# Local attention and two feed-forward networks in one kernel: the low parts of the second network made by VectorE in a written order, and the sigmoid's table loaded at another place

## The chip, the cores and the metric

The kernel runs on one core of a Trainium2 chip. The metric is the device time of one launch in microseconds, as the median of several runs. One execution was also recorded by the hardware profiler; its times are counted from the start of its span.

## The reference, cut to what matters

Attention over 512 local and 32 global positions of 4 batches and 8 heads is followed by two feed-forward networks. The first has a layer norm, a hidden layer of 2048 with ReLU and a residual. The second is this:

```python
def _moe2_ref(x, w_in, conv_w, w_out):          # x (4, 544, 512)
    h = np.maximum(x @ w_in, 0.0)               # (4, 544, 1024)
    hp = pad(h, 1 position at each end)
    conv_out = sum(conv_w[k] * hp[:, k:k + S, :] for k in range(3))
    gate = 1.0 / (1.0 + np.exp(-conv_out))
    return h * gate @ w_out                     # (4, 544, 512)
```

All is in 32-bit floats. The kernel's attention yields 544 positions a batch (`S`), the global ones first.

## The kernel before, in words

Products on TensorE use operands that are split in two: a high part, which is a rounded copy, and a low part, the remainder. Three products (high by high, high by low, low by high) replace one. The helper `split(hi, lo, src, e_hi, e_lo)` (L112) makes both: a copy on engine `e_hi` (ScalarE throughout the second network, L108) and a subtraction on engine `e_lo` (L115). The low parts are the subject here.

The work runs in three stages that overlap: attention, the first network (over chunks of positions, `first_network`, L694) and, from about 540 us, the second network. The first network's hidden products are L711, their ReLU copies `hh` L720 (ScalarE) and `hl` L721 (VectorE), and its output products L735 to L740. While its last chunk runs, the second network's weights are prepared: `narrow` (L124) turns 64-bit words into floats with one Prelu on ScalarE (L131) and two operations on VectorE, and `w1_pair` (L795) forms sums and high and low parts of them.

The second network takes each batch's input `y` (512 features by 544 positions) from memory (`y_load`, into tile `yT`). The first product, `x @ w_in`, is done by a scheme with seven products for eight: features and positions are cut in halves, `y_sums` (L903) makes four sums on VectorE, and `y_split` (L915) splits seven operands, named B11, T2, T3, T1, T4, B21 and B22, into tiles `yc`. The operands T3, T4 and B22 get their low parts from GpSimd, the others from VectorE.

The 1024 hidden features are 8 blocks `f` of 128; two blocks, an even (E) and an odd one (O), are a pair `p`, four pairs a batch (`NPR`). `hidden(b, p, at)` (L1022) works on one pair, n = 4b + p. TensorE makes seven products of six matmuls each (L1005) into the PSUM banks `px`, `py`, `pv` and `pz`, each bank twice or so in a pair. ScalarE copies the first (`p1s`, L1037), VectorE adds the others up (L1032: `u2`, `u3`, and `e1`, `e0`, `o1`, which are the halves of the hidden tiles `he` and `ho`). An addition must have read a bank before TensorE's next product may write there. ScalarE does ReLUs (`relu0`, `relu`, `relu1`).

`gate(b, f, h, e)` (L1007) then does for each block: tap 0 on ScalarE (L1009, named `tap`), taps 1 and 2 on VectorE (L1011, named `(1, b, f)` and `(2, b, f)`), the sigmoid on ScalarE (L1013, `sig`), the product with h on VectorE (L1014, `mul`), and the split into `gh` (ScalarE) and `gl` (engine `e`: GpSimd, and VectorE in the very last pair). GpSimd copies the first 32 columns of both aside (L1018, L1019). There are two buffers `c`, four `gh` and four `gl`. `output` (L1089) multiplies gh and gl by `w_out` (L1077 to L1079), four tiles of twelve matmuls in all for each block; the blocks of pair n are multiplied while pair n + 2 is worked on, after its fourth product and after its seventh. The first two pairs have no such products beside them. At the end of a batch TensorE's results go through ScalarE to memory (L1098).

What sets the order: TensorE executes in the order in which the code is written (`keep_order`). On the other engines a scheduler picks, by priorities that follow the order of the code and by its own estimates of times; `ahead(n)` raises a priority, and `HEAD` (L779) is a list of names whose instructions must follow each other in that order, one list for VectorE and one for ScalarE. Instructions that the list does not name may come between. The four sums of the next batch are named `("sum", b, k)`, and the transposes of the first network's last two result tiles (VectorE, L688) `("turn", (3, 2))` and `("turn", (3, 3))`; each transpose is followed by four stores on SP's queue (L692) to the scratch memory from which batch 3's `y` is read.

The sigmoid needs another table on ScalarE than the functions before it. A sigmoid of one element, `sgd` (L1103), brings the load of that table to a chosen place: behind the last Prelu (`mark["prelu"]`).

Of the kernel before, what the change touches and what calls it, by code (L numbers as in the profile page):

```python
# [12 lines left out]
AF = mybir.ActivationFunctionType  # L13
ALU = mybir.AluOpType
# [4 lines left out]
B, H, SL, SG, D = 4, 8, 512, 32, 64  # L19
# [3 lines left out]
NF, NF2, NDC = FF // P, F2 // P, DM // P  # L23
# [40 lines left out]
def f32(ap):  # L64
    return ap.bitcast(F32)
# [3 lines left out]
def tile_kernel(ctx: ExitStack, tc: tile.TileContext, a_w, a_x, a_e, a_m, g_qk, g_v, w12, g_ln, w_in, w_out, conv_w, out):  # L69
# [42 lines left out]
    def split(hi, lo, src, e_hi, e_lo):  # L112

        copy(e_hi, hi, src)
        e_lo.tensor_tensor(lo, src, f32(hi), op=ALU.subtract)  # L115


    wt, wraw = {}, {}
    mark = {}

    def behind(e):

        return tc.issue_after(mark[e]) if e in mark else nullcontext()
# [319 lines left out]
    order, tiles = [], []  # L443
# [318 lines left out]
    def tick(k):  # L762
# [7 lines left out]
        if ci == 0:  # L770
# [5 lines left out]

    B_ADD = 300
    E0, O0, E1, O1, E2 = ((0, f) for f in range(5))
    HEAD = [  # L779
        [("u3", 0), ("e1", 0), ("e0", 0), ("o1", 0), (1, *E0), ("u2", 1), (2, *E0), ("u3", 1), ("e1", 1), (1, *O0),  # L780
         ("mul", *E0), ("e0", 1), ("turn", (3, 2)), (2, *O0), ("o1", 1), ("mul", *O0), ("turn", (3, 3)), ("u2", 2), (1, *E1), ("u3", 2), ("e1", 2), (2, *E1),
         (1, *O1), ("mul", *E1), ("e0", 2), ("sum", 0, 3), (2, *O1), ("sum", 0, 2), ("o1", 2), ("sum", 0, 1), ("mul", *O1),
         ("sum", 0, 0), (1, *E2), ("u2", 3), (2, *E2), ("u3", 3), ("e1", 3), ("mul", *E2)],
        [("p1s", 0), ("relu0", 0), ("relu", 0), ("tap", *E0), ("p1s", 1), ("relu1", 0), ("tap", *O0), ("sig", *E0),
         ("relu0", 1), ("relu", 1)],
    ]
    NPR = NF2 // 2
    EIGHTH = NDC * P // 2
    HB = S // 2
    zpools = []  # L790
# [4 lines left out]
    def w1_pair(p, home, raw, ab, sums, e):  # L795

        odd, even = 2 * p + 1, 2 * p
        st = {}
        cols = {odd: slice(0, DM), even: slice(DM, 2 * DM)}

        def load(f):
            st[f] = raw(f)
            SP.dma_start(st[f], w_in[f].bitcast(I32))

        def start(f):
            if f == odd:
                st["ab"] = ab()
            fp = st["ab"][:, cols[f]]
            st["o", f] = narrow(fp, st.pop(f), fp)
            mark["prelu"] = st["o", f][0]().ins  # L810

        def homes():
            st["s"] = sums()
            a, x = home()
            wae.append(a)
            wx.append(x)

        def sum_(k):
            a11, a12, a21, a22 = (st["ab"][:, i * EIGHTH:(i + 1) * EIGHTH] for i in range(4))
            s3, s2, s4 = (st["s"][:, i * EIGHTH:(i + 1) * EIGHTH] for i in range(3))  # L820
            o, i0, i1, op = [(s3, a11, a21, ALU.subtract), (a21, a21, a22, ALU.add), (s2, a22, s3, ALU.subtract),
                             (s4, a12, s2, ALU.subtract)][k]
            e.tensor_tensor(o, i0, i1, op=op)

        def hi(w, src, c):
            return lambda: ACT.activation(w[p][:, 0, c], st[src][:, c], AF.Copy)

        def lo(w, src, c, e):
            return lambda: e.tensor_tensor(w[p][:, 1, c], st[src][:, c], f32(w[p][:, 0, c]), op=ALU.subtract)

        a, b, x = cols[odd], cols[even], slice(0, 3 * EIGHTH)
        convs = [[lambda f=f: start(f)] + [lambda f=f, k=k: st["o", f][k]() for k in (1, 2)] for f in (odd, even)]
        rest = [homes, lambda: sum_(0), hi(wae, "ab", a), lambda: sum_(1), lambda: sum_(2), lo(wae, "ab", a, DVE),
                lambda: sum_(3), hi(wae, "ab", b), hi(wx, "s", x), lo(wae, "ab", b, DVE), lo(wx, "s", x, e)]
        return lambda f: lambda: load(f), convs, rest
# [76 lines left out]
                lambda: DVE.tensor_tensor(b12, b12, b11, op=ALU.subtract),  # L912
                lambda: DVE.tensor_tensor(t4, b21, t2, op=ALU.subtract)]

    def y_split(n):  # L915
        split(*yc[n], ysrc[n], ACT, POOL if Y_NAMES.index(n) in (2, 4, 6) else DVE)


    free = "xe" if last % 2 else "xo"
# [12 lines left out]

    def y0_split(n):
        y_home(n)
        y_split(n)

    raws = []

# [65 lines left out]
                with behind(key):  # L1004
                    PE.matmul(ps, wx_, y[:, d], start=start and d + m == 0, stop=d + m == 3, skip_group_check=True)  # L1005

    def gate(b, f, h, e):  # L1007
        c = gpool.tile([P, S], F32, tag="c", name="c")
        named["tap", b, f] = ACT.activation(c, h[:, 0:S], AF.Copy, scale=cw[:, 3 * f:3 * f + 1])  # L1009
        for k in (1, 2):  # L1010
            named[k, b, f] = DVE.scalar_tensor_tensor(c, h[:, k:S + k], cw[:, 3 * f + k:3 * f + k + 1], c, op0=ALU.mult,  # L1011
                                                      op1=ALU.add)
        named["sig", b, f] = ACT.activation(c, c, AF.Sigmoid)  # L1013
        named["mul", b, f] = DVE.tensor_tensor(c, h[:, 1:S + 1], c, op=ALU.mult)  # L1014
        gh = gpool.tile([P, S], F32R, tag="gh", name="gh", bufs=4)
        gl = gpool.tile([P, S], F32R, tag="gl", name="gl", bufs=4)
        split(gh, gl, c, ACT, e)
        POOL.tensor_copy(grem_h[:, f, b * SG:(b + 1) * SG], f32(gh[:, :SG]))  # L1018
        POOL.tensor_copy(grem_l[:, f, b * SG:(b + 1) * SG], f32(gl[:, :SG]))  # L1019
        gts[b, f] = gh, gl  # L1020

    def hidden(b, p, at):  # L1022

        a, x = wae[p], wx[p]
        n = b * NPR + p
        he, ho = hs[2 * n % 4], hs[(2 * n + 1) % 4]
        p1s, u2, u3 = (us[:, n % 2 * 3 + i] for i in range(3))
        e = DVE if n == B * NPR - 1 else POOL

        def add(name, o, i0, i1):  # L1030
            with ahead(B_ADD):
                named[name, n] = DVE.tensor_tensor(o, i0, i1, op=ALU.add)  # L1032

        px = ps_x.tile([P, HB], F32, tag="px", name="px")
        product(px, a, 0, "B11", True, "first")
        with ahead(B_ADD):
            named["p1s", n] = ACT.activation(p1s, px, AF.Copy)  # L1037
        at("B11")
        py = ps_x.tile([P, HB], F32, tag="py", name="py")
        product(py, x, 1, "T2", True, "first")  # L1040
        add("u2", u2, py, p1s)
        at("T2")
        pv = ps_v.tile([P, HB], F32, tag="pv", name="pv")
        product(pv, x, 0, "T3", True)
        add("u3", u3, pv, u2)
        at("T3")
        pz = ps_v.tile([P, HB], F32, tag="pz", name="pz")
        product(pz, a, 2, "T1", True)
        add("e1", he[:, U1], pz, u3)
        at("T1")  # L1050
        at(0)

        def t4():
            product(pv, a, 3, "T4", False)
            add("e0", he[:, U0], pv, u2)
            named["relu", n] = ACT.activation(he[:, 1:1 + S], he[:, 1:1 + S], AF.Relu)
            at("T4")

        def b21():
            product(px, a, 1, "B21", False)  # L1060
            with ahead(B_ADD):
                named["relu0", n] = ACT.activation(ho[:, U0], px, AF.Relu)
            at("B21")

        for part in (b21, t4) if n < 2 else (t4, b21):
            part()
        gate(b, 2 * p, he, e)
        product(pz, x, 2, "B22", False)
        add("o1", ho[:, U1], pz, u2)
        named["relu1", n] = ACT.activation(ho[:, U1], ho[:, U1], AF.Relu)  # L1070
        at("B22")
        gate(b, 2 * p + 1, ho, e)
        at(1)

    def mm_o(o, gh, gl, f, first, last):
# [23 lines left out]

    steps = [(b, f) for b in range(B) for f in range(NF2)]  # L1100
    second = len(traced())
    with behind("prelu"):
        ACT.activation(sgd, mhalf, AF.Sigmoid)  # L1103
    gpool.tile([P, S], F32R, tag="gl", name="gl", bufs=4)
    yT, sums = None, []
    for i in range(B * NPR):
        b, p = divmod(i, NPR)
        if p == 0 and b + 1 < B:
            yT = [(gpool.tile([P, NDC, S], F32, tag="yT", name="yT", bufs=1), slice(0, NDC))]
            y_load(b + 1, yT)  # L1110
        if p == 2 and b + 1 < B:
            sums = y_sums(yT, yt)

        def at(n):
            if n in (0, 1):
                if 2 * i >= 4:
                    output(*steps[2 * i - 4 + n])
            else:
                for _ in range(len(sums) if p == NPR - 1 else min(len(sums), 1)):
                    named["sum", b, len(sums)] = sums.pop(0)()  # L1120
                if b + 1 < B and p == NPR - 1:
                    y_split(n)

        hidden(b, p, at)
    for st in steps[-4:-1]:
# [6 lines left out]
        (ACT if b % 2 else SP).dma_start(out[b, :SG, :], orem[b * SG:(b + 1) * SG])  # L1132
    output(*steps[-1])
    keep_order(second, [mybir.EngineType.PE])
    for order in HEAD + [[("e0", NPR * b + 2), ("sum", b, 3)] for b in range(1, B - 1)]:
        order = [named[k].ins for k in order]
        for one, two in zip(order, order[1:]):
            tc.add_manual_dep(two, one.name, mybir.DependencyInfo(
                mybir.DependencyClass.NoSync, mybir.DependencyReason.DATA), reason="order")
# [103 lines left out]
```

## Time and profile before

| what | value |
|---|---|
| time, median of 3 runs | 736.89 us (736.3 to 737.52) |
| profiled execution, its own time | 736.67 us |
| its span, first to last instruction | 734.9 us |
| TensorE busy | 717.2 us (98% of the span) |
| VectorE busy | 497.0 us (68%) |
| ScalarE busy | 399.4 us (54%) |
| GpSimd busy | 241.3 us (33%) |

In the rows of the profile PE is TensorE's matmuls, PEld its weight loads, DVE VectorE, ACT ScalarE, POOL GpSimd, and SPq the queue of SyncE, which only issues transfers. In rows of busy time by stretch the engines stand in the order PE, PEld, DVE, ACT, POOL. An arrow reads "written from". A bracket at a row's end is the idle time of the engine ahead of it and what ended that.

### The profile page before, as it was taken

Reading aid. Unit: us, or ns where it says so; the run is one execution under the profiler, and the core shown is the slowest. Engines: PE = TensorE matmul, PEld = TensorE weight load, DVE = VectorE, ACT = ScalarE, POOL = GpSimd, SP = SyncE. Lnnn points to the kernel's source line nnn. Section 1 sums busy time; section 2 is a strip of 40 time slices with the busy share of each in tenths; the row PEclk is TensorE's granted clock in tenths of the full one; section 3 lists DMA queues with packets and bytes.
Section 4 is the critical chain, followed back from the end, with each engine's and each line's share of the span. In section 5 each row is a group of like instructions: output and inputs, shape, how many; then the busy total and the mean of one; then the engine's idle time right before and its main releaser. Section 6 shows DMA issues by size and latency. Waiting matters only on the chain.

```text
span 734.9 us, 12936 instructions
## 1 busy us (share of the span) xinstructions
PE 717.2 (98%) x4665; PEld 642.9 (87%) x4665; DVE 497.0 (68%) x1108; ACT 399.4 (54%) x927; POOL 241.3 (33%) x287
## 2 busy tenths in 40 slices
PE   9989999999999999999999999999999899999997
PEld 5878799999999999999999999989988788998886
DVE  3889982857677676756557534744859978778661
ACT  5858653455565656545445531523655576466551
POOL 1012031334354543434324410001343745417320
PEclk9999999999999999999999999999999999999999
DMA  9992231532443353243224102307311110110102
GB/s 370 425 415 85 71 136 52 110 98 84 117 106 97 98 126 104 87 124 93 83 74 108 44 23 32 112 30 235 141 62 30 62 57 1 62 58 1 59 0 72
DMA packets 64160, 76.19 MB, mean 104 GB/s; under 512 B 39120, under 2 KB 46048, under 8 KB 61536
## 3 DMA queue, kind: packets, MB, share of 16 engines
q1 hardware_dynamic: 31888, 70.59, 28.8%
q10 hardware_dynamic: 32208, 4.77, 3.9%
q8 instruction: 37, 0.61, 0.3%
q14 instruction: 27, 0.22, 0.1%
HBM read 66.43 MB, written 8.91 MB: 103 GB/s over the span
## 4 chain that ended last, share of the span: by engine, by line
PE 75%; DVE 15%; issue 4%; ACT 3%; DMA 3%; ACTq 0%; SPq 0%; DVEq 0%
PE ph L711 21%; PE yps L735 7%; PE yps L736 7%; PE yps L740 7%; PE po L337 3%; PE pt L316 3%; DVE c L1011 3%; PE po L1078 3%; PE po L1077 3%; PE po L1079 3%; PE pz L1005 2%; PE pv L1005 2%; DMA wraw<-w_in 2%; PE px L1005 2%; PE pog L422 1%
## 5 line engine op out<-in xcount | busy, mean ns | idle before, releaser
L711 PE MATMUL ph<-xe,w 128*128 128x256 f32 (+1 forms) x768 | 119.4, 298 | 0.9 <-ACT w L159 0.9
L711 PEld LDWEIGHTS ph<-xe,w 128*128 128x128 f32 x768 | 108.9, 188 | 6.7 <-ACT w L159 1.2
L115 POOL TENSOR_TENSOR kl<-raw,kh 128x448 fp32r<-128x448 f32 (+2 forms) x59 | 70.0, 1186 | 131.0 <-ACT kh L108 124.3
L735 PE MATMUL yps<-w,hh 128*128 128x512 f32 x272 | 110.2, 405 | 2.4 <-ACT hh L720 1.8
L711 PE MATMUL ph<-xo,w 128*128 128x256 f32 x768 | 108.6, 285 | 0.0
L736 PE MATMUL yps<-w,hh 128*128 128x512 f32 x272 | 107.8, 396 | 0.0
L711 PEld LDWEIGHTS ph<-xo,w 128*128 128x128 f32 x768 | 101.7, 190 | 4.4
L720 ACT ACTIVATE hh<-ph 128x256 fp32r<-128x256 f32 (+1 forms) x128 | 50.3, 394 | 70.6 <-PE ph L711 54.4
L721 DVE SCALAR_TENSOR_TENSOR hl<-ph,hh 128x256 fp32r<-128x256 f32 x112 | 46.4, 416 | 49.5 <-ACT hh L720 49.0
L740 PE MATMUL yps<-w,hl 128*128 128x512 f32 x224 | 73.0, 400 | 0.0
L294 DVE CUSTOM_DVE_ANT_0 sm<-ps,mask 128x192 f32<-128x192 f32 (+1 forms) x128 | 42.5, 368 | 36.4 <-PE ps L291 24.8
L115 POOL TENSOR_TENSOR gl<-c,gh 128x544 fp32r<-128x544 f32 x30 | 43.2, 1439 | 70.8 <-ACT gh L108 61.0
L303 ACT ACTIVATE sm<-sm,nm 128x192 f32<-128x192 f32 (+1 forms) x128 | 58.7, 460 | 12.4 <-DVE nm L294 12.1
L1011 DVE SCALAR_TENSOR_TENSOR c<-hs,cw,c 128x544 f32<-128x544 f32 x64 | 58.3, 935 | 3.3 <-ACT c L1009 2.0
L735 PEld LDWEIGHTS yps<-w,hh 128*128 128x128 f32 x272 | 51.2, 188 | 9.5 <-ACT hh L720 2.8
L736 PEld LDWEIGHTS yps<-w,hh 128*128 128x128 f32 x272 | 51.4, 189 | 5.5
L108 ACT ACTIVATE kh<-raw 128x448 fp32r<-128x448 f32 (+2 forms) x59 | 34.3, 582 | 39.6 <-issue 17.1
L1078 PE MATMUL po<-w,gh 128*128 128x512 f32 x128 | 50.7, 396 | 0.0
L1077 PE MATMUL po<-w,gh 128*128 128x512 f32 x128 | 50.6, 395 | 0.0
L1079 PE MATMUL po<-w,gl 128*128 128x512 f32 x128 | 50.5, 395 | 0.0
L261 POOL TENSOR_TENSOR qs<-raw,qs 64x256 fp32r<-64x256 f32 x43 | 33.6, 783 | 46.3 <-DVE qs L260 21.2
L740 PEld LDWEIGHTS yps<-w,hl 128*128 128x128 f32 x224 | 41.0, 189 | 8.6 <-DVE hl L721 0.3
(187 smaller groups left out, 1503.8 us busy)
## 6 DMA issues: line engine op xcount, KB each, us to landing
wraw<-w SPq DMA_DIRECT2D x16, 1024.0 KB, 16.9
raw<-a_m SPq DMA_DIRECT2D x23, 352.0 KB, 3.0
raw<-a_e SPq DMA_DIRECT2D x20, 320.0 KB, 2.9
raw<-g_qk SPq DMA_DIRECT2D x16, 304.0 KB, 2.8
rawg<-g_v SPq DMA_DIRECT2D x16, 280.0 KB, 2.9
wraw<-w_in SPq DMA_DIRECT2D x8, 512.0 KB, 6.2
wraw<-w_out SPq DMA_DIRECT2D x4, 1024.0 KB, 7.6
raw<-a_w SPq DMA_DIRECT2D x4, 912.0 KB, 9.7
```

Of the source, the lines that this page charges most:

```text
L115: e_lo.tensor_tensor(lo, src, f32(hi), op=ALU.subtract)
L303: ACT.activation(s, s, AF.Exp, bias=self.nm[:, j:j + 1], scale=-1.0, accum_out=xt.sums[:, h:h + 1])
L711: e = PE.matmul(ph[:, :n], w[:, d * P:(d + 1) * P], x[:, d], start=m == 0, stop=m == 3 * NDC - 1)
L720: ACT.activation(hh, ph[:, :n], AF.Relu)
L721: DVE.scalar_tensor_tensor(hl, ph[:, :n], 0.0, f32(hh), op0=ALU.max, op1=ALU.subtract)
L735: PE.matmul(yps[i], hh[:, tk], wh[:, DM:], start=edge(k, -1), stop=False)
L736: PE.matmul(yps[i], hh[:, tk], wl[:, DM:], start=False, stop=False)
L740: mark["last"] = PE.matmul(yps[i], hl[:, tk], wh[:, DM:], start=False, stop=edge(k, 1)).ins
L1011: named[k, b, f] = DVE.scalar_tensor_tensor(c, h[:, k:S + k], cw[:, 3 * f + k:3 * f + k + 1], c, op0=ALU.mult, op1=ALU.add)
L1077: PE.matmul(o, gh, wh, start=first, stop=False)
L1078: PE.matmul(o, gh, wl, start=False, stop=False)
L1079: PE.matmul(o, gl, wh, start=False, stop=last)
```

## The change

The low parts of the second network's gates and of its `yc` operands for batches 1 to 3 all go to VectorE; batch 0's `yc`, made during the first network, stay as they were. `HEAD` is written anew: VectorE's list names the low parts (`lo`) of the first four blocks, puts `u3` right behind `u2` and `o1` right behind `e0`, and the two transposes move to a list of their own, behind `e0` of pairs 5 and 6. For batches 1 and 2 two short lists put `yc` T3 and the product of block 4 behind `u3` and `e1` of the batch's last pair. The one-element sigmoid is no longer tied to the last Prelu; ScalarE's list puts it between `p1s` and `relu0` of pair 0.

```diff
@@ split
-        e_lo.tensor_tensor(lo, src, f32(hi), op=ALU.subtract)
+        return e_lo.tensor_tensor(lo, src, f32(hi), op=ALU.subtract)
@@ HEAD
+    NPR = NF2 // 2
     HEAD = [
-        [("u3", 0), ("e1", 0), ("e0", 0), ("o1", 0), (1, *E0), ("u2", 1), (2, *E0), ("u3", 1), ("e1", 1), (1, *O0),
-         ("mul", *E0), ("e0", 1), ("turn", (3, 2)), (2, *O0), ("o1", 1), ("mul", *O0), ("turn", (3, 3)), ("u2", 2), (1, *E1), ("u3", 2), ("e1", 2), (2, *E1),
-         (1, *O1), ("mul", *E1), ("e0", 2), ("sum", 0, 3), (2, *O1), ("sum", 0, 2), ("o1", 2), ("sum", 0, 1), ("mul", *O1),
-         ("sum", 0, 0), (1, *E2), ("u2", 3), (2, *E2), ("u3", 3), ("e1", 3), ("mul", *E2)],
-        [("p1s", 0), ("relu0", 0), ("relu", 0), ("tap", *E0), ("p1s", 1), ("relu1", 0), ("tap", *O0), ("sig", *E0),
+        [("u3", 0), ("e1", 0), ("e0", 0), ("o1", 0), (1, *E0), ("u2", 1), ("u3", 1), (2, *E0), ("e1", 1), (1, *O0),
+         ("mul", *E0), ("e0", 1), ("o1", 1), (2, *O0), ("lo", *E0), ("u2", 2), ("u3", 2), ("mul", *O0), ("e1", 2),
+         (1, *E1), (2, *E1), ("lo", *O0), (1, *O1), ("mul", *E1), ("e0", 2), (2, *O1), ("sum", 0, 3), ("o1", 2),
+         ("lo", *E1), ("sum", 0, 2), ("mul", *O1), ("sum", 0, 1), ("sum", 0, 0), ("u2", 3), ("u3", 3), (1, *E2), ("e1", 3),
+         (2, *E2), ("lo", *O1)],
+        [("p1s", 0), ("sgd",), ("relu0", 0), ("relu", 0), ("tap", *E0), ("p1s", 1), ("relu1", 0), ("tap", *O0), ("sig", *E0),
          ("relu0", 1), ("relu", 1)],
+        [("e0", NPR + 1), ("turn", (3, 2)), ("e0", NPR + 2), ("turn", (3, 3))],
     ]
@@ w1_pair
-            mark["prelu"] = st["o", f][0]().ins
+            st["o", f][0]()
@@ y_split, y0_split
-    def y_split(n):
-        split(*yc[n], ysrc[n], ACT, POOL if Y_NAMES.index(n) in (2, 4, 6) else DVE)
+    def y_split(n, e=DVE):
+        return split(*yc[n], ysrc[n], ACT, e)
...
-        y_split(n)
+        y_split(n, POOL if Y_NAMES.index(n) in (2, 4, 6) else DVE)
@@ gate, hidden
-    def gate(b, f, h, e):
+    def gate(b, f, h):
...
-        split(gh, gl, c, ACT, e)
+        named["lo", b, f] = split(gh, gl, c, ACT, DVE)
...
-        e = DVE if n == B * NPR - 1 else POOL
...
-        gate(b, 2 * p, he, e)
+        gate(b, 2 * p, he)
...
-        gate(b, 2 * p + 1, ho, e)
+        gate(b, 2 * p + 1, ho)
@@ the loop over pairs
-    with behind("prelu"):
-        ACT.activation(sgd, mhalf, AF.Sigmoid)
+    named["sgd",] = ACT.activation(sgd, mhalf, AF.Sigmoid)
...
-                    y_split(n)
+                    named["yc", b, n] = y_split(n)
...
-    for order in HEAD + [[("e0", NPR * b + 2), ("sum", b, 3)] for b in range(1, B - 1)]:
+    for order in HEAD + [[("e0", NPR * b + 2), ("sum", b, 3)] for b in range(1, B - 1)] + [
+            [("u3", NPR * b + 3), ("e1", NPR * b + 3), e] for b in range(1, B - 1) for e in (("yc", b, "T3"), ("mul", b, 4))]:
```

## Rows read from the trace of the kernel before

**Rows 1.** Busy time by stretch: start:end, length, engines (instructions), granted clock, DMA share, GB/s.

```profile
549.50:580.00 30.50, 26.50 (x164) 23.30 (x163) 29.87 (x42) 19.06 (x36) 14.92 (x15) 1.00 0.12 18
```

**Rows 2.** TensorE's waits from 515 to 735: us in total, times, longest.

```profile
PE pv L1005 <- DVE us L1032: 3.1, 2, 2.7
PE pz L1005 <- DVE hs L1032: 2.9, 3, 1.0
```

**Rows 3.** Timeline around the table load: start, duration, engine, line, operation.

```profile
533.74 1.28 ACT L1103 ACT_TABLE_LOAD   x1
...
535.14 0.36 ACT L720 ACTIVATE hh<-ph 128x256 fp32r<-128x256 f32 x1
...
535.56 0.50 PE L735 MATMUL yps<-w,hh 128*128 128x512 f32 x1 [1.79 <-ACT hh L720]
```

**Rows 4.** Timeline of TensorE: the first product of pairs 2, 4, 8, 11 and 12.

```profile
553.36 0.92 PE L1005 MATMUL px<-yc,wae 128*128 128x272 f32 x6
...
580.09 0.92 PE L1005 MATMUL px<-yc,wae 128*128 128x272 f32 x6
...
625.34 0.91 PE L1005 MATMUL px<-yc,wae 128*128 128x272 f32 x6
...
658.09 0.91 PE L1005 MATMUL px<-yc,wae 128*128 128x272 f32 x6
...
670.24 0.91 PE L1005 MATMUL px<-yc,wae 128*128 128x272 f32 x6
```

**Rows 5.** Busy time by stretch, behind the idle time of rows 3.

```profile
536.00:540.00 4.00, 4.00 (x18) 3.58 (x17) 2.61 (x3) 1.07 (x4) 3.87 (x8) 0.57 0.01 2
```

**Rows 6.** Timeline of GpSimd, VectorE and TensorE around 554 to 557.

```profile
554.34 1.36 POOL L115 TENSOR_TENSOR gl<-c,gh 128x544 fp32r<-128x544 f32 x1 [9.79 <-PE px L1005]
...
554.46 1.82 DVE L1011 SCALAR_TENSOR_TENSOR c<-hs,cw,c 128x544 f32<-128x544 f32 x1
...
556.20 0.43 DVE L1032 TENSOR_TENSOR hs<-pz,us 128x272 f32<-128x272 f32 x1
...
556.68 1.01 PE L1005 MATMUL pz<-yc,wae 128*128 128x272 f32 x6 [0.90 <-DVE hs L1032]
```

**Rows 7.** Timeline of VectorE and TensorE around 572 to 575.

```profile
572.50 1.85 DVE L1011 SCALAR_TENSOR_TENSOR c<-hs,cw,c 128x544 f32<-128x544 f32 x1
...
574.75 1.03 PE L1005 MATMUL pv<-yc,wae 128*128 128x272 f32 x6 [2.70 <-DVE us L1032]
```

**Rows 8.** Timeline of ScalarE in pair 0: `p1s` and `relu0`.

```profile
542.52 0.38 ACT L1037 ACTIVATE us<-px 128x272 f32<-128x272 f32 x1
546.75 0.40 ACT L1062 ACTIVATE hs<-px 128x272 f32<-128x272 f32 x1 [3.85 <-PE px L1005]
```

**Rows 9.** Instructions on tile `c`: count, ns min/median/max, first and last start, form.

```profile
L1011 DVE SCALAR_TENSOR_TENSOR c<-hs,cw,c x64: 772/784/1900, 549.5 to 714.2; 128x544 f32<-128x544 f32 x64
...
L108 ACT ACTIVATE gh<-c x32: 642/659/685, 553.6 to 716.5; 128x544 fp32r<-128x544 f32 x32
L115 POOL TENSOR_TENSOR gl<-c,gh x30: 1352/1367/1862, 554.3 to 707.2; 128x544 fp32r<-128x544 f32 x30
L115 DVE TENSOR_TENSOR gl<-c,gh x2: 719/722/726, 716.3 to 717.2; 128x544 fp32r<-128x544 f32 x2
```

**Rows 10.** Groups of VectorE in 549.5 to 580: count, busy us, mean ns, idle before.

```profile
L1011 DVE SCALAR_TENSOR_TENSOR c<-hs,cw,c 128x544 f32<-128x544 f32 x12 | 14.4, 1203 | 0.8 <-ACT c L1009 0.8
```

**Rows 11.** Timeline of VectorE at the end of batch 1.

```profile
619.40 1.88 DVE L115 TENSOR_TENSOR yc<-yT,yc 128x544 fp32r<-128x544 f32 x1
621.21 0.43 DVE L1032 TENSOR_TENSOR hs<-pz,us 128x272 f32<-128x272 f32 x1
```

**Rows 12.** Timeline of SP's queue: stores of y, stores of the output, load of batch 3.

```profile
554.57 5.74 SPq L692 DMA_DIRECT2D yscr<-x  x8
...
601.11 2.98 SPq L1098 DMA_DIRECT2D out<-osb  x4
626.82 0.38 SPq L888 DMA_DIRECT2D yT<-yscr  x1
```

More of the change, by code (lines that the diff above doesn't have):

```diff
@@ L778, in tile_kernel @@
     E0, O0, E1, O1, E2 = ((0, f) for f in range(5))
+    NPR = NF2 // 2
     HEAD = [
-        [("u3", 0), ("e1", 0), ("e0", 0), ("o1", 0), (1, *E0), ("u2", 1), (2, *E0), ("u3", 1), ("e1", 1), (1, *O0),
-         ("mul", *E0), ("e0", 1), ("turn", (3, 2)), (2, *O0), ("o1", 1), ("mul", *O0), ("turn", (3, 3)), ("u2", 2), (1, *E1), ("u3", 2), ("e1", 2), (2, *E1),
-         (1, *O1), ("mul", *E1), ("e0", 2), ("sum", 0, 3), (2, *O1), ("sum", 0, 2), ("o1", 2), ("sum", 0, 1), ("mul", *O1),
-         ("sum", 0, 0), (1, *E2), ("u2", 3), (2, *E2), ("u3", 3), ("e1", 3), ("mul", *E2)],
-        [("p1s", 0), ("relu0", 0), ("relu", 0), ("tap", *E0), ("p1s", 1), ("relu1", 0), ("tap", *O0), ("sig", *E0),
+        [("u3", 0), ("e1", 0), ("e0", 0), ("o1", 0), (1, *E0), ("u2", 1), ("u3", 1), (2, *E0), ("e1", 1), (1, *O0),
[4 more added lines that the diff above has]
+        [("p1s", 0), ("sgd",), ("relu0", 0), ("relu", 0), ("tap", *E0), ("p1s", 1), ("relu1", 0), ("tap", *O0), ("sig", *E0),
          ("relu0", 1), ("relu", 1)],
+        [("e0", NPR + 1), ("turn", (3, 2)), ("e0", NPR + 2), ("turn", (3, 3))],
     ]
-    NPR = NF2 // 2
     EIGHTH = NDC * P // 2
```

## The prediction

> **What bounds the kernel now.** I read the busy shares in stretches first. TensorE is the engine that counts: it has no free stretch except around the start of the second network. In 549.5 to 580 it is busy 26.50 of 30.50 us, while VectorE is busy 29.87 of them [rows 1]: there VectorE sets the pace. Then TensorE's waits from 515 on: five for VectorE, 6.0 us together, two before `pv` and three before `pz` [rows 2]. Those are PSUM banks that an addition of `hidden` has not yet read. A sixth, for ScalarE, stands ahead of the second network [rows 3]. The timeline then says what each addition stood behind.
>
> TensorE's own steady pace is the yardstick. From 625.34 to 658.09 three pairs pass with no wait: 10.92 us a pair [rows 4]. Against it, pairs 2 and 3 (553.36 to 580.09) take 26.73 instead of 21.83, 4.9 too many; pairs 4 to 7 (580.09 to 625.34) 45.25 instead of 43.67, 1.6 too many; pair 11 (658.09 to 670.24) 12.15, 1.2 too many [rows 4]. These 7.7 us contain the five waits and the restart of the pipeline behind each. With what the sixth wait costs, this is all that a better order on the other engines could win.
>
> **The table load.** ScalarE loads the sigmoid's table from 533.74; the ReLU copy `hh` that TensorE needs next starts at 535.14 and TensorE goes on at 535.56, after 1.79 us idle [rows 3]. Without the load `hh` can start at 533.74: **1.40 us** less, and 0.39 us of idle time stays, since a Prelu ahead of it is late anyway. [...]
>
> The load goes behind `p1s` of pair 0. There ScalarE has nothing from 542.90 to 546.75, when `relu0` gets its operand: 3.85 us of cover [rows 8] for 1.40. [...] Without cover it would cost its 1.40 before `relu0`.
>
> [...]
>
> [...]
>
> **Low parts from GpSimd to VectorE.** 30 `gl` at 1.37 us on GpSimd become 30 at 0.72 on VectorE [rows 9]; nine `yc` low parts have the same shape, so the same price. That adds 39 x 0.72 = 28 us to VectorE. What comes back: taps (`scalar_tensor_tensor`) take 0.78 undisturbed and up to 1.90 [rows 9]. The row to look at is the tap at 554.46: 1.82 us, behind a GpSimd subtraction that began at 554.34 and ran 1.36 [rows 6]. [...] In 549.5 to 580 twelve taps take 1.20 on the mean [rows 10], 12 x 0.42 = 5.0 us too many. Added in the same stretch are five `gl` (E0 to E2) and about two `yc`: 7 x 0.72 = 5.0 us. So even in the worst stretch the balance is nil before the two transposes that leave it, and GpSimd keeps only its short copies of 32 columns. VectorE's load over a batch: a pair has 5 additions of 0.43 [rows 6], 4 taps of 0.78, two low parts of 0.72 and two products of the same shape [rows 9], 8.15 us; a batch adds four sums and seven `yc`, 7.9: 4 x 8.15 + 7.9 = 40.5 against TensorE's 43.7. It fits. What the move costs on the path is nothing by this; it is covered by TensorE's own products.
>
> A low part now stands in VectorE's queue behind a copy `gh` of 0.66 us [rows 9], and behind it wait the additions that free TensorE's banks. The written order puts other work between product and low part; only in `lo O0`, then tap 1 of O1, a hand-over to ScalarE and back is open (the tap needs the buffer that `lo` frees): about 0.75 us, at a point where the next addition is due some 2 us later. I charge nothing, at most 0.9.
>
> **The written order.** Each wait of rows 2 has its cause in what stands before an addition, and the new list takes it away.
> - `o1` of pair 1 ends at 556.63, TensorE waits 0.90 [rows 6]. In front of it stood a transpose and the slow tap; now it follows `e0` directly, at least the tap's 1.82 us earlier.
> - `u3` of pair 3: TensorE waits 2.70 at 574.75; before it stood a tap of 1.85 [rows 7] and two `yc` low parts. Now `u3` is named right behind `u2`, and the taps come after. The 0.4 us wait (the other `pv` of rows 2) has the same form.
> - In batches 1 and 2 `e1` of the last pair stands behind a `yc` low part of 1.88 [rows 11], which itself was stretched by GpSimd. Now `e1` follows `u3`, and `yc` T3 and the product of feature block 4 come after: 1.2 us at each of the two.
> So 4.9 + 1.6 + 1.2 = **7.7 us** go. What is late next is TensorE itself, at 10.92 us a pair. Not named are the other `yc` low parts at the three batch ends; they may still stand before an addition. Bounds: 0 to 1.2 each (the present wait); I take 0.3, **0.9** together.
>
> **The transposes of the last two y tiles** go to pairs 5 and 6, with eight stores on SP's queue that now start at 554.57. Near 601 they meet four output stores; the load that reads them is issued at 626.82 [rows 12]. VectorE has room there, and some 15 us remain: nothing on the path. Without those 15 us batch 3's load would be late, and behind it its sums and TensorE's first product of that batch.
>
> **The sum.** Profiled execution 736.67 us (span 734.9, 1.8 around it). 1.40 + 1.7 + 7.7 = 10.8 at most; less 0.35 and 0.9, 9.6. So 727.1, and as the median is 0.2 above the profiled time, **727.3 us**.
>
> **Rivals.**
> - A, the forecast: 727.3; by itself 725.5 to 729.5.
> - B, waits at the batch ends stay: low parts that the list doesn't name slip before `u3` of pair 3 and before `e1`. For it: VectorE is full there [rows 1] and seven `yc` are in one queue now. Against it: with GpSimd quiet each of them is 0.72. It keeps 2.7 + 2.4 of the waits: 727.3 + 5.1 - 0.9 = 731.5.
> [...]
> - D, slower: VectorE is saturated and the moved work shows. Then the long taps are not GpSimd's doing, or its small copies stretch them as much. It decides where the taps' mean in the first batch stays near 1.20. [...] Against it: the tap and the subtraction of rows 6 lie on each other to a tenth. [...]
> [...]
>
> **How the numbers follow.** A 0.58, B 0.22, C 0.08, D 0.06, E 0.06. What this kernel's measurement can tell from no change is 0.2%, 1.5 us. Faster: A, B and C, 0.88; same: E, 0.06; slower: D, 0.06. The range reaches from the whole 10.8 us with a little more from short copies (725.5) past B (732.5); outside lie D, E and the edge of B.
>
> **What would show it.** Right: no table load near 534, `hh` by 533.8, granted clock 1.00 in 530 to 545; the table load between `p1s` and `relu0`; taps near 0.78; GpSimd with 32-column copies only; pair to pair 10.92 from pair 2 on; no wait over 0.5 before `pv` or `pz`. Wrong: VectorE idle for ScalarE before low parts, taps still above 1 us, or a first-batch pair above 11.5 us. The prediction fails most simply if the low parts' order at the batch ends, which nothing names, puts a bank's addition last.

## The result and the profile after

The changed kernel takes 727.13 us (median of 4 runs, 726.36 to 727.54); before 736.6 in the runs beside it. The ratio is 0.9876, 95% interval 0.985 to 0.9901: 1.2% faster. The forecast was 727.3. The span of the profiled execution went from 734.9 to 725.3 us.

TensorE's waits from 515 on, after (us in total, times, longest); they answer to [rows 2, 3]:

```profile
PE yps L735 <- ACT hh L720: 0.3, 1, 0.3
PE pv L1007 <- DVE us L1033: 0.2, 1, 0.2
```

The five waits for VectorE are gone, and a new one of 0.2 us stands in pair 0. The place of the table load, in the timeline after [rows 3, 8]:

```profile
534.64 0.50 PE L735 MATMUL yps<-w,hh 128*128 128x512 f32 x1 [0.29 <-ACT hh L720]
...
541.95 0.38 ACT L1038 ACTIVATE us<-px 128x272 f32<-128x272 f32 x1
542.35 1.28 ACT L1103 ACT_TABLE_LOAD   x1
...
544.36 0.40 ACT L1063 ACTIVATE hs<-px 128x272 f32<-128x272 f32 x1 [0.50 <-PE px L1007]
```

The idle time ahead of `yps` is 0.29 instead of 1.79 us, and the table load ends in time for `relu0`, with 0.50 us to spare. Busy time by stretch, after (start:end, length, PE, PEld, DVE, ACT, POOL, granted clock, DMA share, GB/s):

```profile
536.00:540.00 4.00, 4.00 (x28) 3.69 (x27) 2.18 (x4) 0.80 (x2) 3.29 (x9) 1.00 0.01 2
545.00:576.00 31.00, 31.00 (x206) 28.53 (x205) 28.12 (x52) 20.92 (x39) 5.49 (x10) 1.00 0.08 26
```

The clock behind the idle time is 1.00, where it was 0.57 [rows 5]. In the middle of those 4 us it was 0.50, the half clock of the texts below; busy time by stretch, before:

```profile
536.50:539.50 3.00, 3.00 (x12) 2.67 (x11) 2.11 (x3) 0.35 (x2) 3.00 (x7) 0.50 0.01 3
```

Worked out from [rows 5], 4 us at 0.57 cost 4 x 0.43 = 1.7 us, an estimate. After, TensorE is busy throughout the first batch, and VectorE, with all the low parts, 28.12 of 31 us, against 29.87 of 30.5 [rows 1]. The two stretches do not hold the same work (52 and 42 instructions). From 560 to 576 VectorE is busy without a break; 0.88 us of its idle time before that is one wait, for ScalarE, ahead of tap 1 of O1 in the timeline after:

```profile
558.66 0.78 DVE L1013 SCALAR_TENSOR_TENSOR c<-hs,cw,c 128x544 f32<-128x544 f32 x1 [0.88 <-ACT c L1011]
```

This is the hand-over behind `lo` of O0, of which the prediction said 0.75 us and charged nothing. TensorE has no wait there. Instructions on tile `c` after (ns min/median/max), which answer to [rows 9]:

```profile
L1013 DVE SCALAR_TENSOR_TENSOR c<-hs,cw,c x64: 769/781/795, 547.6 to 704.6; 128x544 f32<-128x544 f32 x64
```

The median of the taps was 784 before and is 781, but the longest was 1900 and is 795. In the timeline of before ten of the 64 taps take more than 1 us, from 1.35 to 1.90, and each of the ten starts after a GpSimd subtraction (L115) has begun and has subtractions beside it for 0.77 to 1.59 us [rows 6, 7]; so has the `yc` low part of 1.88 us at the end of batch 1 [rows 11], by the first row below. Two taps started 0.1 us ahead of a subtraction: these took 0.77 us, and the subtraction 1.89, as in the other rows. Timeline of GpSimd and VectorE, before:

```profile
618.86 1.84 POOL L115 TENSOR_TENSOR gl<-c,gh 128x544 fp32r<-128x544 f32 x1
...
669.70 0.77 DVE L1011 SCALAR_TENSOR_TENSOR c<-hs,cw,c 128x544 f32<-128x544 f32 x1
...
669.80 1.89 POOL L115 TENSOR_TENSOR yc<-yT,yc 128x544 fp32r<-128x544 f32 x1
```

After, the last subtraction of GpSimd starts at 535.21, ahead of the taps.

To see where the time came from I take two marks on TensorE: the start of the hidden products (L711) ahead of the late `hh`, at 532.19 before and 532.77 after, and the start of the last pair's `py`, at 703.74 and 694.12. Between them lie 171.55 and 161.35 us: 10.20 less. The table gives the stretch from the first mark to `py` of pair 0, and then the distances from `py` to `py` by pair, for all kernels of this study; each is the difference of two starts in the timeline.

| kernel | to pair 0 | pair 0 | 1 | 2 | 3 | 4 to 6 | 7 | 11 | mark to mark |
|---|---|---|---|---|---|---|---|---|---|
| before | 9.97 | 6.63 | 5.33 | 12.71 | 14.02 | 33.10 | 12.14 | 12.15 | 171.55 |
| the change | 7.00 | 7.13 | 5.26 | 10.91 | 11.09 | 32.75 | 10.85 | 10.86 | 161.35 |
| the change again | 7.01 | 7.08 | 5.26 | 10.91 | 11.10 | 32.75 | 10.85 | 10.86 | 161.32 |
| table only | 7.01 | 7.08 | 5.32 | 12.73 | 15.37 | 32.71 | 12.15 | 12.16 | 169.96 |
| all but the table | 9.97 | 6.63 | 5.27 | 10.91 | 11.11 | 32.75 | 10.86 | 10.86 | 163.86 |
| engine only, with table | 7.03 | 7.09 | 5.30 | 11.31 | 12.53 | 32.71 | 10.86 | 10.86 | 163.18 |
| order only, with table | 7.05 | 7.05 | 5.27 | 10.91 | 12.14 | 34.19 | 10.86 | 10.86 | 163.82 |
| yc on GpSimd | 7.06 | 7.08 | 5.28 | 10.91 | 12.38 | 32.75 | 10.86 | 10.85 | 162.67 |
| transposes back | 7.02 | 7.07 | 5.28 | 11.01 | 12.80 | 32.66 | 10.83 | 10.82 | 162.81 |
| transposes back, yc behind e1 | 7.06 | 7.07 | 5.28 | 10.96 | 12.69 | 32.87 | 10.83 | 10.83 | 162.91 |
| three table loads | 7.02 | 8.27 | 5.30 | 10.91 | 10.86 | 32.75 | 10.86 | 10.86 | 162.32 |
| low parts twice | 7.04 | 7.08 | 5.28 | 10.91 | 16.15 | 32.75 | 11.11 | 10.98 | 166.76 |
| two early copies | 6.38 | 7.12 | 5.28 | 10.91 | 11.08 | 32.75 | 10.86 | 10.85 | 160.73 |
| all three orders | 6.38 | 7.12 | 5.28 | 10.90 | 11.28 | 32.95 | 10.86 | 10.86 | 161.13 |

The times of these kernels differ by less than their spread in most cases; the marks repeat to 0.03 us (the change and the change again), so verdicts on a microsecond rest on them. They are one profiled execution of each kernel, and a fall of the clock between the marks counts in them: there is one in before, table only, all but the table and low parts twice, and none in the others. They leave out what lies ahead of the first mark: that mark comes at 531.49 to 534.30 us, in a part that the change doesn't touch. One cause shows in the timelines: a wait for `hh` in the first network, absent before, 0.47 us in the change (at 508.44) and 1.73 us in the change's second profile:

```profile
505.60 0.50 PE L735 MATMUL yps<-w,hh 128*128 128x512 f32 x1 [1.73 <-ACT hh L720]
```

### The profile page after: what moved, and what is told of

Its sections match the earlier page's. It is cut to its first block, busy times and chain, and to the rows that moved or that the text cites. A ratio compares the mean times of both kernels' runs of the same rounds, so it can differ in the third digit from the quotient of the medians.

```text
span 725.3 us, 12952 instructions
## 1 busy us (share of the span) xinstructions
PE 714.7 (99%) x4665; PEld 641.6 (88%) x4665; DVE 500.9 (69%) x1147; ACT 400.4 (55%) x927; POOL 189.1 (26%) x248
## 4 chain that ended last, share of the span: by engine, by line
PE 86%; DVE 6%; ACT 2%; DMA 2%; issue 2%; POOL 1%; ACTq 0%; DVEq 0%
PE ph L711 23%; PE yps L735 7%; PE yps L740 7%; PE yps L736 7%; PE po L1079 4%; PE po L1080 4%; PE po L1078 4%; PE pz L1007 3%; PE pv L1007 3%; PE px L1007 3%; PE po L337 3%; PE pt L316 3%; PE py L1007 2%; PE pog L422 1%; PE ps L291 1%
## 5 line engine op out<-in xcount | busy, mean ns | idle before, releaser
L711 PE MATMUL ph<-xe,w 128*128 128x256 f32 (+1 forms) x768 | 119.5, 298 | 0.9 <-ACT w L159 0.9
L711 PEld LDWEIGHTS ph<-xe,w 128*128 128x128 f32 x768 | 108.9, 188 | 6.7 <-ACT w L159 1.2
L711 PE MATMUL ph<-xo,w 128*128 128x256 f32 x768 | 107.8, 284 | 0.0
L711 PEld LDWEIGHTS ph<-xo,w 128*128 128x128 f32 x768 | 100.8, 188 | 4.3
L115 POOL TENSOR_TENSOR kl<-raw,kh 128x448 fp32r<-128x448 f32 (+2 forms) x59 | 70.1, 1188 | 131.0 <-ACT kh L108 124.0
L1013 DVE SCALAR_TENSOR_TENSOR c<-hs,cw,c 128x544 f32<-128x544 f32 x64 | 49.0, 781 | 3.7 <-ACT c L1011 2.8
L321 ACT ACTIVATE ptsb<-pt 128x384 f32<-128x384 f32 (+1 forms) x64 | 34.5, 540 | 22.1 <-PE pt L316 21.4
```

The lines of the kernel that those rows point to most:

```text
L115: return e_lo.tensor_tensor(lo, src, f32(hi), op=ALU.subtract)
L711: e = PE.matmul(ph[:, :n], w[:, d * P:(d + 1) * P], x[:, d], start=m == 0, stop=m == 3 * NDC - 1)
```

## The experiments

**Table only and all but the table.** The first is the kernel before with

```diff
-    with behind("prelu"):
-        ACT.activation(sgd, mhalf, AF.Sigmoid)
+    named["sgd",] = ACT.activation(sgd, mhalf, AF.Sigmoid)
...
-        [("p1s", 0), ("relu0", 0),
+        [("p1s", 0), ("sgd",), ("relu0", 0),
```

and the second is the changed kernel with these lines as they were.

> The kernel before with only the table load moved behind p1s of pair 0. Theory (three separate gains): the idle time at the last chunk falls from 1.79 to about 0.4 us, the granted clock stays at 1.00 behind it, and 1.40 + 1.7 less 0.35 = 2.7 us go, in which the five waits of the second network stay as they are (6.0 us in all). Rival (VectorE sets the pace of the first batch anyway, so that TensorE's earlier start is eaten by longer waits there): under 1 us goes, and the wait before pv in pair 3 grows from 2.7 to about 5. Rival on the clock: it falls all the same, 1.0 us goes.

> The changed kernel with the table load back behind the last Prelu. Theory: the idle time of 1.8 us and the half clock behind it are back, the five waits stay away: 7 us faster than before, 2.5 to 3 slower than the whole change. Rival (the two parts need each other): less than 5 us faster than before. If the clock is 1.00 behind an idle time of 1.8 us, the fall before was chance and not the idle time's doing.

Table only: 735.05 us, ratio 0.9967 (0.9948 to 0.9986). The start wins 2.96 us as said, but only 1.59 are left at the second mark. 0.45 go in pair 0, and 1.35 in pair 3, whose wait is no longer than before (2.69 against 2.70). What is new there is the clock. Timeline and busy time by stretch of this kernel:

```profile
571.54 1.06 PE L1005 MATMUL pv<-yc,wae 128*128 128x272 f32 x6 [2.69 <-DVE us L1032]
```

```profile
572.00:576.00 4.00, 4.00 (x20) 3.86 (x19) 4.00 (x8) 2.66 (x6) 2.08 (x2) 0.57 0.00 0
```

So neither theory nor rival had it: longer waits for VectorE ate nothing, a fall of the clock did, at another idle time than the one removed. All but the table: 728.8 us, ratio 0.9884 (0.986 to 0.9909); the pairs' part falls from 161.58 to 153.89 us (`py` of pair 0 to `py` of pair 15), 7.7, and the idle time of 1.79 us is back, with 9.97 us to pair 0 as before. The table's place is worth 163.86 - 161.35 = 2.5 us on top in these two profiles. The times hardly show it: 728.8 against 727.13 us, in separate sets of runs, with ratios of 0.9884 and 0.9876 to before. The clock is one reason. Of the six executions of all but the table, three have a mean granted clock of 0.998, among them the profiled one with its single fall, and three of 1.000. Four us at 0.57 lower the mean of 727 us by 0.002, so there is no room for that fall in those three (no trace of them is kept). The fall of the clock, by the estimate 1.7 of the 2.5 us, then came in some executions and not in others. The kernel before varies too, from 0.993 to 1.000 over 31 executions.

**Engine only and order only.** Both have the table load at its new place. Engine only is the changed kernel with VectorE's list of before and without the lists for the batch ends; order only is the changed kernel with

```diff
-        named["lo", b, f] = split(gh, gl, c, ACT, DVE)
+        split(gh, gl, c, ACT, DVE if b == B - 1 and f >= NF2 - 2 else POOL)
...
-                    named["yc", b, n] = y_split(n)
+                    y_split(n, POOL if Y_NAMES.index(n) in (2, 4, 6) else DVE)
```

and the low parts taken out of the lists.

> All low parts on VectorE and the table load at its new place, but the list of before (transposes in it, u3 behind a tap, no low part named, no lists at the batch ends). Theory (the long taps are GpSimd's doing): taps at 0.78 us, and of the waits of 7.7 us most goes although the order is the old one: 4 to 7 us of the 7.7, so 7 to 9 us faster than before. Rival (it is the written order that does it): 2.7 us from the table alone, the waits stay at 5 us or more.

> The new list, the transposes moved and the table load at its new place, but all low parts on the engines of before (GpSimd for gl and for T3, T4, B22), their names taken out of the list. Theory (contention and order each do a part): taps still up to 1.9 us, mean near 1.2 in the first batch; o1 and u3 come at once, so the waits of 0.9, 0.4 and 2.7 shrink, but VectorE is as full as before and they come back later, 2 to 4 us of the 7.7 left: 6 to 8 us faster than before. Rival (order does all): no wait is left, 9.5 us faster. Rival (engine does all): 3 us faster.

Engine only: 727.87 us, ratio 0.9872 (0.9847 to 0.9897); order only: 729.94, ratio 0.9893 (0.9869 to 0.9916). Groups of VectorE in 545 to 576 (count, busy, mean ns), first engine only, then order only:

```profile
L1011 DVE SCALAR_TENSOR_TENSOR c<-hs,cw,c 128x544 f32<-128x544 f32 x12 | 9.3, 779 | 0.8 <-ACT c L1009 0.8
```

```profile
L1013 DVE SCALAR_TENSOR_TENSOR c<-hs,cw,c 128x544 f32<-128x544 f32 x12 | 12.9, 1078 | 2.2 <-ACT c L1011 2.2
```

The long taps go with GpSimd's subtractions and not with the order: without them the taps take 0.78 us in the old order as in the new, with them 1.20 in the old [rows 10] and 1.08 in the new. Mark to mark, with the 2.5 us of the table taken off, engine only wins 171.55 - 163.18 - 2.5 = 5.9 of the 7.7 us and order only 5.2. Against table only, where the clock falls in pair 3, it is 6.8 and 6.1 of 8.6 us. The two don't add up; each alone takes away most of the same waits. What each leaves is different. Engine only still waits 1.41 us before `pv` of pair 3, behind the old order. Order only waits for an addition in pair 3 (0.69 us) and, in pair 4, for a cast (0.27 us) and for a low part that GpSimd makes, in its timeline:

```profile
578.60 0.50 PE L1080 MATMUL po<-w,gl 128*128 128x512 f32 x1 [0.70 <-POOL gl L115]
```

The batch ends (pairs 7 and 11) are at 10.86 in both: there either part is enough.

**The yc low parts on GpSimd.** The changed kernel with the second edit of order only, and `gl` on VectorE.

> The changed kernel with the low parts of T3, T4 and B22 back on GpSimd for batches 1 to 3; gl stay on VectorE. Theory (what counts is whether a GpSimd subtraction lies on a tap or a low part ahead of an addition): three subtractions a batch end stretch VectorE by up to 3 x 1.1 us there, which the lists keep away from u3 and e1 in batches 1 and 2; pairs 7 and 11 stay at 10.9 us, pair 3 (no list) may lose up to 1 us. Total 0 to 1 us slower than the change. Rival (each GpSimd subtraction costs TensorE its length): 3 us slower or more.

727.97 us; 1.3 us more mark to mark, all of it in pair 3. That is a little over what was expected, and at another place: an output product waits 1.01 us for `gl` of O1, since that subtraction took 1.88 us beside one of GpSimd's. The three lines of its timeline:

```profile
570.05 1.81 POOL L115 TENSOR_TENSOR yc<-yt,yc 128x544 fp32r<-128x544 f32 x1 [1.03 <-ACT yc L108]
...
570.57 1.88 DVE L115 TENSOR_TENSOR gl<-c,gh 128x544 fp32r<-128x544 f32 x1
...
572.50 0.50 PE L1080 MATMUL po<-w,gl 128*128 128x512 f32 x1 [1.01 <-DVE gl L115]
```

**The transposes back.** The changed kernel with

```diff
-         ("mul", *E0), ("e0", 1), ("o1", 1), (2, *O0), ("lo", *E0), ("u2", 2), ("u3", 2), ("mul", *O0), ("e1", 2),
+         ("mul", *E0), ("e0", 1), ("turn", (3, 2)), (2, *O0), ("o1", 1), ("lo", *E0), ("u2", 2), ("u3", 2), ("mul", *O0), ("turn", (3, 3)), ("e1", 2),
...
-        [("e0", NPR + 1), ("turn", (3, 2)), ("e0", NPR + 2), ("turn", (3, 3))],
```

and then the same with one more line, which keeps the `yc` low parts of batch 0 from standing before `u3` and `e1` of pair 3:

```diff
+    HEAD += [[("e1", 3), ("yc", 0, n)] for n in Y_NAMES]
```

> The changed kernel with the two transposes back in the first batch: one ahead of tap 2 of O0, with o1 of pair 1 behind both, one behind the product of O0. Theory (order is of little matter once GpSimd is quiet): o1 of pair 1 comes 1.4 us later than in the change and still in time or 0.4 us late; total 0 to 0.5 us slower. Rival (the first batch has no room on VectorE for two more instructions, and they come back as waits): 1.3 us or more slower in pairs 2 and 3.

> The transposes back in the first batch (as in the run before, which lost 1.9 us in pair 3), and all yc low parts of batch 0 named behind e1 of pair 3. Theory (the loss is rival B's: low parts that no list names stand between u2 and u3 of pair 3, 2.2 us of them; the transposes only used up the slack): the wait of 1.7 us before pv goes, pair 3 at 11.0 or below. Rival (the transposes themselves are too much for VectorE in the first batch): pair 3 stays above 12 us, the wait is before pv, pz or an output product instead.

The theory fell twice. `o1` of pair 1 is in time, but pair 3 takes 12.80 us, 1.7 more than in the change, for two instructions of 0.70 us. In the change the margin there is small: what stands behind `u2` of pair 3 up to `u3`, and the product that follows, in the timeline after:

```profile
565.58 0.71 DVE L115 TENSOR_TENSOR yc<-yT,yc 128x544 fp32r<-128x544 f32 x1
566.21 1.35 DVE L115 TENSOR_TENSOR yc<-hs,yc 128x544 fp32r<-128x544 f32 x2
567.48 0.43 DVE L1033 TENSOR_TENSOR us<-pv,us 128x272 f32<-128x272 f32 x1
...
568.13 0.92 PE L1007 MATMUL pv<-yc,wae 128*128 128x272 f32 x6
```

`u3` ends at 567.91 and TensorE starts 0.2 us later: 1.9 us of low parts that no list names stand between `u2` and `u3`, and fit by that much. With the transposes they don't. But keeping those low parts behind `e1` doesn't help, it only moves the wait. The waits for VectorE of the two kernels, transposes back first (both also have the 0.2 us in pair 0):

```profile
PE pv L1006 <- DVE us L1032: 1.9, 2, 1.7
```

```profile
PE po L1079 <- DVE gl L115: 1.6, 1, 1.6
```

So holding back the `yc` low parts isn't the cure: from tap 1 of O1 on VectorE is hardly idle in either kernel, and what is moved comes back at another product. That no order has room for the two transposes isn't shown. In both, VectorE stands idle for 1.17 us ahead of that tap (at 561.63 and 559.59), for ScalarE, at the hand-over of the change's 0.88 us, and a transpose of 0.70 us in that place wasn't tried.

Engine only and transposes back differ in VectorE's order alone: 163.18 and 162.81 us mark to mark. With GpSimd quiet and the transposes in the first batch, the written order proper is worth 0.4 us.

**Three table loads.** The changed kernel with an exponential and a second sigmoid of one element behind the first, each with its own load (1.28 us each, at 541.39, 542.91 and 544.42).

> The changed kernel with three table loads (sigmoid, exponential, sigmoid) where it has one, between p1s and relu0 of pair 0: 2 x 1.5 = 3.0 us more on ScalarE. Theory (the cover there is 2.0 us, of which one load takes 1.5): relu0 is 2.5 us late, the bank px is asked for again 1.4 us after relu0 would have freed it, so TensorE waits about 1 us in pair 1, and with the taps late 1 to 2 us go in all. Rival (the cover is the 3.85 us of the profile of before): less than 0.7 us.

727.15 us; the wait is where it was expected, ahead of the first product of pair 1 (the table counts it in pair 0, which runs to `py` of pair 1), in the timeline of this kernel:

```profile
546.26 1.04 PE L1007 MATMUL px<-yc,wae 128*128 128x272 f32 x6 [0.92 <-ACT hs L1063]
```

Mark to mark it costs 0.97 us (1.14 in pair 0, and 0.23 come back in pair 3): the cover is about 2 us, not the 3.85 of the profile before, and one load fits.

**Low parts twice.** Each `gl` subtraction is made a second time; nothing else differs from the change.

> The changed kernel with each of the 32 gl subtractions made twice on VectorE: 32 x 0.64 us (start to start) more, 1.3 us a pair. Theory (VectorE has room in a steady pair, none in the first batch): pairs 8 to 10 and 12 to 14 stay at 10.9 us; in the first batch four or five more subtractions stand before u3 of pair 3, so that TensorE waits about 3 us there; batch ends lose at most 1 us each. Total 3 to 5 us slower than the change. Rival D of the prediction (VectorE saturated, each instruction there shows): 20 us slower. Rival (room everywhere): under 1 us.

731.39 us, ratio 0.9947 (0.9932 to 0.9962) to before; 4.6 us more than the change again, which ran beside it, and 5.4 us more mark to mark, 5.1 of them in pair 3: a wait of 3.20 us before `pv`, as expected, and behind it the clock falls, which wasn't. Timeline and busy time by stretch:

```profile
570.53 1.60 PE L1007 MATMUL pv<-yc,wae 128*128 128x272 f32 x6 [3.20 <-DVE us L1034]
```

```profile
571.00:575.00 4.00, 4.00 (x21) 3.92 (x20) 4.00 (x8) 2.83 (x6) 0.21 (x1) 0.61 0.00 0
```

Steady pairs stay at 10.9 us and the batch ends lose 0.1 to 0.3. VectorE has room in the later batches and none in the first one. Rival D, a VectorE that is full throughout, said 20 us and doesn't hold.

**Two early copies, all three orders, the change again.** Two early copies adds to the change two short lists for ScalarE, with names for the instructions concerned; all three orders has the line on `yc` behind `e1` as well.

```diff
+        [("hh", NF - 3), ("pre", 2 * NPR - 1)], [("p1s", 0), ("hi", NPR - 1, "s")],
```

> The changed kernel with two places on ScalarE put right: hh of the third last hidden block ahead of the Prelu that waits for VectorE, and p1s of pair 0 ahead of the copy of the last pair's weights. Theory (what the change still loses against TensorE's own pace is these two waits): the waits of 0.29 and 0.21 us and the slow restart behind each go, 0.7 to 1 us less from the last hidden products to the end. Rival (the loss of pair 0 lies in VectorE's two residual operations): 0.3 us.

> The changed kernel (transposes late) with the two early copies on ScalarE and the yc low parts of batch 0 behind e1 of pair 3. From the last hidden products on, 0.6 us less by the early copies and up to 0.2 in pair 3: 0.8 us less than the change, which the times can hardly show. Rival (yc late delays the next batch's first product): pair 4 starts late, no gain.

> The change itself, to be compared with the runs beside it on the same chip: as before, waits of 0.3 and 0.2 us only, 161.35 us from the last hidden products to the first of the last pair's second products, within 0.1.

Two early copies: 726.42 us, 160.73 mark to mark, 0.6 less than the change, all at the idle time of 0.29 us, which is gone. The slow restart shows in the timeline after: the matmul behind those 0.29 us takes 0.50 us and the next 0.39, the product behind the 0.21 us in pair 0 takes 1.01 and the next 0.92. The wait in pair 0 is gone too, but pair 0 is as long as before (7.12): another of 0.17 us for an `hh` has come ahead of it. All three orders: 726.2 us, 161.13, only 0.2 less than the change, since the late `yc` cost 0.4 in pairs 3 to 6; that expectation failed. Neither can be told from the change (726.78 in the runs beside the second) by its time.

## Why the prediction was right, point by point

- **The table load.** Idle time 1.50 us shorter (1.40 said), no fall of the clock behind 0.29 us: 9.97 - 7.00 = 3.0 us, for 1.4 + 1.7 = 3.1. No run shows the 1.7 by itself: what the runs showed in its place is a clock of 1.00 instead of 0.57 [rows 5] and 2.97 - 1.50 = 1.47 us. The 3.0 are shown by the two pairs of kernels that differ in it alone, in their profiles; the 1.7 us of the fall are not lost in each execution (three of six of all but the table had none), which the prediction took for granted. Of the cover of 3.85 us [rows 8], 2.0 were there.
- **`p1s` late in pair 0.** 0.35 charged, a guess that no run shows; the runs showed 0.5 in its place (7.13 against 6.63).
- **The waits of the second network.** 7.7 said, 7.7 measured with the table at its old place. The first product behind a wait takes 1.01 or 1.03 us [rows 6, 7] and a product without one 0.91 or 0.92 [rows 4], so 0.1 of each restart shows. The mechanism holds as well: taps at 0.78, `u3` and `e1` in time, batch ends at 10.86.
- **VectorE's room.** The taps gave back what was worked out, 12 x 0.42 = 5.0 us (0.78 instead of 1.20). Whether the balance was nil can't be read off, as the two stretches hold different work. But the move costs nothing on the path only because 1.4 us of transposes leave the first batch, and their leaving had no term in the sum: put back, they cost 1.5 us mark to mark. The open hand-over behind `lo` of O0 is there, 0.88 us, and costs VectorE time ahead of its full stretch, but no wait of TensorE by itself.
- **Unnamed low parts.** Rival B's mechanism is there, at the one end where no list guards: three `yc` low parts before `u3` of pair 3. They fit by 0.2 us, and `pv` starts without idle time. Pair 3 still takes 11.09 instead of 10.92: behind `pv`, a `pz` starts 0.06 us after its addition ends (569.59, with a fourth `yc` low part ahead of it), and an output product 0.06 us after its `gl` (570.92), and both are 0.1 us longer than elsewhere. So of the 0.9 charged 0.2 at most was taken. The batch ends with lists took none.
- **The sum.** 10.8 less 0.35 and 0.9 was 9.6; the span fell by 9.6. That close an agreement is luck: mark to mark it was 10.2, the charge on the batch ends being too high, and 0.6 was lost ahead of the first mark, where the change has no part.
- **The stores** of the late transposes start at 592.20 and 603.12, the load of batch 3 is issued at 618.15: 13 us between the last store's issue and the load, 15 said. No wait came of it.

What isn't settled is how engine and order divide the gain, because they don't divide: each alone wins 5.2 to 5.9 of 7.7 us. Order only has both the new list and the late transposes, and late transposes alone weren't run, so the share of each is open.

## What to carry to other kernels

When a slower engine's work (1.37 us a low part against 0.72 [rows 9]) lies on a busy engine's instructions (the tap of 1.82 us under a subtraction of 1.36 [rows 6]), moving that work to the busy engine can be free: count what the overlap costs it, not only what the move adds. Where a queue is full only at the start of a stage, look there for what could run later, as the two transposes did, ahead of any fine order. And before costing a repair of one wait, ask what the clock does at the next one: in its profile the table's place alone won 3.0 us and kept 1.6.

## What the runs showed of the hardware

TensorE's granted clock fell behind some idle times and not behind others of about the same length. It fell behind 1.79 us (before, to 0.57 on the mean of 536 to 540 [rows 5], and all but the table, where the mean of the execution is 0.998), 1.76 us (transposes back, in the first network, 0.59 on 506 to 510), 2.69 us (table only, 0.57 on 572 to 576) and 3.20 us (low parts twice, 0.61 on 571 to 575). It stayed at 1.00 behind 2.70 us (before, pair 3, in the 1.00 of [rows 1]), 1.73 (the change again, first network, mean of the execution 1.000) and 1.70 (transposes back, pair 3, 1.00 on 571 to 575). No fall shows behind 1.75 (all but the table, first network: four us at 0.57 make a mean of 0.998, so there is room for one fall, that behind 1.79) and 1.41 (engine only: products of 0.92 us behind it, where table only has 1.55). The 1.76, 1.75 and 1.73 us are one and the same wait in three kernels, and by the mean clocks of the three executions (0.998, 0.998 and 1.000) in none of them had the clock fallen before it. The wait of transposes back and the stretch behind it, which in the change again has a granted clock of 1.00 (505 to 509):

```profile
505.96 0.50 PE L735 MATMUL yps<-w,hh 128*128 128x512 f32 x1 [1.76 <-ACT hh L720]
```

```profile
506.00:510.00 4.00, 4.00 (x16) 3.56 (x17) 2.75 (x6) 2.29 (x5) 0.28 (x1) 0.59 0.44 81
```

So neither the length of the idle time nor an earlier fall tells these apart, and a fall in one profile need not come in the next execution of the same kernel, as the mean clocks of all but the table show (0.998 three times, 1.000 three times). What decides was not found.
